# Six heads of batch 0 by the hardware queues, two by GpSimd's, and a re-ordered opening in a kernel of cross attention and a gated feed-forward layer

## The chip, the cores and the metric

The kernel runs on one core of one Trainium2 chip. The metric is device time in microseconds (us) for one execution. The core has five engines that run their own instruction streams side by side: TensorE (PE: matmuls and transposes), VectorE (DVE), ScalarE (ACT), GpSimd (POOL) and SyncE (SP, which here only issues transfers). Transfers (DMA) are issued by SP and ACT on the hardware queues (hardware_dynamic in the profile) and by POOL on the software queue (software_dynamic). In this kernel only POOL's transfers convert from float32 to bfloat16 on their way.

## What is computed

x is 8 batches x 8 heads x 512 rows x 64, state is 8 x 8 x 32 x 64. Two cross attentions share their scores, and what they give goes through a feed-forward layer with a rectified gate:

```python
scores = scale * np.matmul(x, state.transpose(0, 1, 3, 2))
a = softmax(scores)                       # over the 32 states
xread = np.matmul(a, state)
scores2 = scale * np.matmul(state, x.transpose(0, 1, 3, 2))
a2 = softmax(scores2)                     # over the 512 rows
sread = np.matmul(a2, x)
attn_out = np.concatenate([xread, sread], axis=2)
...
x = attn_out.transpose(0, 2, 1, 3).reshape(B * S, H * D)     # 4352 x 512
gate = np.maximum(x @ w_gate, 0.0)        # 512 x 1536
val = x @ w_val                           # 512 x 1536
return gate * val @ w_out                 # 1536 x 512
```

(softmax stands here for the reference's subtraction of the maximum, exponential and division.)

## The kernel before, in words

A batch's 512 rows lie as 128 partitions x 4 rows, for 8 heads of 64 columns. For each batch the kernel needs xT, the transpose of x in 16 blocks of 128 x 128 (two blocks for each head), and stT, the transposed states. Scores (att_sc, sc.b.jp) are matmuls of xT blocks with stT for four heads at a time, jp = 0 for heads 0 to 3 and jp = 1 for heads 4 to 7. ACT takes the exponential of each (att_exp, ex.b.jp, L206), DVE sums it and takes the reciprocal (att_sum, nr.b.jp, L212 and L214) and scales (att_scale, nx.b.jp, L218). The result is transposed again (aT, copied by ao) to be one operand of the feed-forward matmuls. The other operand is U, the product of state and weights (c_unit, c.b.lo.n for small pieces, copied to U by co at L320), so that gate and val come from one pair of matmuls over U (gv, L325), followed by ACT's rectifier (re, L354), DVE's product (mu, L358) and the output matmuls (o, L367).

The order of the first stretch is written out by hand. The text called program is a list of words, each of which emits the instructions of one step; for each engine they come in the order of the words that use it. A word such as xT.0.8.4@4 means step xT with arguments 0, 8, 4 (batch 0, blocks 8 to 11, that is heads 4 and 5) into PSUM bank 4. The steps that matter here:

- spin.1.n: one matmul of n columns (512 if not given) whose result nobody uses; spin32.2 is two of them in float32 at the very start.
- stc, stT, sto: states to bfloat16 (L118), transpose on PE (L123), copy out (L140).
- xc.0.j.eng: heads 2j and 2j+1 of batch 0 from the float32 tile xf to the bfloat16 tile xb, on engine eng (x_conv_pair, L144).
- xT.b.lo.n: n blocks of xb transposed on PE into PSUM (x_T, L162); xo.b.lo.n.eng: those blocks copied from PSUM to xT on engine eng (x_out, L165).
- sc, ex, nr, nx: as above. dx.b.part.parts: a part of batch b's x by POOL's queue (x_load, L441). dw: a piece of the gate or value weights by POOL's queue (w_dma, L109).

Ahead of the program stand the first transfers: on SP heads 0 and 1 in float32 and then a small one, touch, which reads 96 pieces of 32 bytes out of x into a tile that nothing reads; on ACT the states of the first batches and then heads 2 and 3 in float32; on POOL heads 4 to 7 with conversion, straight into xb. Then POOL makes the identity for the transposes and issues batch 1 in two halves, and after that weights, batch 2, the other states and the output weights. After the program a loop over groups of 128 feed-forward columns runs for the rest of the kernel, which the change leaves alone. The tile hs_sb (spare is its flat view) is first written long after the opening.

Of the kernel before, what the change touches and what calls it, by code (L numbers as in the profile page):

```python
# [8 lines left out]
FP32 = mybir.dt.float32  # L9
# [7 lines left out]
def kernel(  # L17
# [9 lines left out]
    nc = tc.nc  # L27

    B, H, S, D = x.shape
# [4 lines left out]
    NC = S // 128  # L34
# [3 lines left out]
    def pool(name, bufs, space=None):  # L38
        if space is None:
            return ctx.enter_context(tc.tile_pool(name=name, bufs=bufs))  # L40
        return ctx.enter_context(tc.tile_pool(name=name, bufs=bufs, space=space))

    const = pool("const", 1)
    upool = pool("upool", 3)
    xin = pool("xin", 1)
    att = pool("att", 2)
    small = pool("small", 4)
    anspool = pool("anspool", 3)
# [5 lines left out]

    NK = 2
    HK = H // NK


    wg_sb = const.tile([128, NJ, d_ff], BF16, name="wg_sb")
# [12 lines left out]
    spare = hs_sb.rearrange("p f n -> p (f n)")  # L72
# [5 lines left out]
    xf, xb, xT, eT, e_sn, a_sn, ANS, U, hsb = {}, {}, {}, {}, {}, {}, {}, {}, {}  # L78
# [18 lines left out]
    def state_dma(eng, lo, hi):  # L97
        src = state.rearrange("(g b) h (m i) d -> (b h m) g i d", b=2, i=4)
        eng.dma_start(out=st_f[:, lo // 2:hi // 2], in_=src[:, lo // 2:hi // 2])

    def place(h):

        return h // NJ, h % NJ ^ h // NJ

    def xb_alloc(b):
        xb[b] = att.tile([128, H, NC, D], BF16, name="xb", tag="xb", bufs=4)
# [75 lines left out]
    def sT_mm(b):  # L182

        held["sT", b] = [bank("sT_ps"), bank("sT_ps")]
        for kc in range(NK):
            for h in range(HK * kc, HK * kc + HK):
                j = place(h)[1]
# [62 lines left out]
    def x_pad(b):  # L250

        v = xa[:, b % NX].rearrange("p (c h) d -> p h c d", c=NC)[:, :, :, 0:D]
        for hs in (slice(0, HK), slice(HK, H)):
            nc.gpsimd.tensor_copy(out=v[:, hs], in_=xb[b][:, hs])  # L254
# [156 lines left out]

    ctx.enter_context(tc.manual_schedule())
    nc.vector.memset(stT, 0.0)
    xf[0] = xin.tile([128, HK, NC, D], FP32, name="xf", tag="xf")
    touch = const.tile([96, 1, 8], FP32, name="touch")

    def touch_dma(k, src, lo, n, step):
        v = src.rearrange("(a r) c -> a r c", r=step)[lo:lo + n, 0, 0:8]
        nc.sync.dma_start(out=touch[0:n, k], in_=v)

    for eng, j in ((nc.sync, 0), (nc.scalar, None), (nc.scalar, 1)):
        if j is None:
            state_dma(eng, 0, 2)
        else:
            src = x[0, 2 * j:2 * j + 2].rearrange("h (p c) d -> p h c d", c=NC)
            eng.dma_start(out=xf[0][:, 2 * j:2 * j + 2], in_=src)
    touch_dma(0, x.rearrange("b h s d -> (b h s) d"), 32, 96, 64)
    nc.scalar.activation(out=tiny, in_=nc.const_aps.tensor(0.0, (128, 1), FP32), func=AF.Exp)

    def w_load(w, lo, n):  # L430
        w_dma((moe_w_gate, moe_w_val)[w], (wg_sb, wv_sb)[w], lo, lo + n)

    xb_alloc(0)
    nc.gpsimd.dma_start(out=xb[0][:, HK:H], in_=x[0, HK:H].rearrange("h (p c) d -> p h c d", c=NC))
    make_identity(nc, id128)

    def x_load(b, part, parts):
# [13 lines left out]
    def x_load_behind(b, gb, gj):  # L451
# [11 lines left out]
    dx.1.0.2 dx.1.1.2 stc.0.1.dve stc.0.0.dve dw.0.0.128 dw.1.0.128 dw.0.128.128 dw.1.128.128 dw.0.256.256  # L463
    dw.1.256.256 dw.0.512.256 spin32.2 stT.0@0 dw.1.512.256 dw.0.768.256 dw.1.768.256 dw.0.1024.256 dw.1.1024.256
    dw.0.1280.256 dw.1.1280.256 dx.2.0.1 ds do.0.6 xc.0.0.act spin.1.256 xT.0.0.4@1 xc.0.1.dve sto.0.0.act
    spin.1.128 xT.0.4.4@2 xo.0.0.4.dve sto.0.1.dve xo.0.4.4.act spin.1 sc.0.0@3 ex.0.0 nr.0.0 spin.1.384
        xT.0.8.4@4 xT.0.12.4@5 xo.0.8.4.act xo.0.12.4.act spin.1 xT.1.0.8@6 sc.0.1@1 ex.0.1 xo.1.0.8.dve spin.1
    sc.1.0@0 xT.1.8.8@2 stc.1.1.pool stc.1.0.pool do.6.12 spin.1 c.0.0.128@34 nx.0.0 ex.1.0 nr.0.1 xo.1.8.8.act on
    stc.2.0.pool stc.3.1.pool co.0.0.128.0.act co.0.0.128.1.act spin.1 sc.1.1@5 nx.0.1 nr.1.0 aT.0.1@6 aT.0.0@1
    ex.1.1 c.1.128.128@02 ao.0.0.dve ao.0.1.act c.0.128.128@34 c.1.0.128@51 co.0.128.128.0.act gv.0.0@63  # L470
    co.1.128.128.1.act co.0.128.128.1.act re.0.0 co.1.128.128.0.act gv.0.1@72 nr.1.1 nx.1.0 co.1.0.128.1.act re.0.1
# [89 lines left out]
    for g in range(first, NF * (B + 1)):  # L561
        b, jf = divmod(g, NF)
# [47 lines left out]
```

## Time and profile before

| What | us |
|---|---|
| Three timed runs | 219.24, 220.28, 220.39 (median 220.28) |
| The profiled execution | 219.11 |
| its span, first to last instruction | 217.3 |
| PE busy | 209.4 |
| DVE busy | 134.8 |
| ACT busy | 117.8 |
| POOL busy | 42.5 |

The page of the profile gives busy times and shares of the span, the chain that ended last (followed back from the last instruction to what released it), the costliest groups of instructions, and for each transfer the time from its issue to its landing. In a timeline each line is: start, length, engine, line of the code, operation, out<-in, shapes, count; in brackets the engine's idle time before it and what ended it. An ended wait for several things is put down to the last of them. Lines such as L165 belong to a helper that several steps share. The granted clock of PE over the span was 0.998 of full speed.

### The profile page before, as it was taken

Reading aid. Unit: us, or ns where it says so; the run is one execution under the profiler, and the core shown is the slowest. Engines: PE = TensorE matmul, PEld = TensorE weight load, DVE = VectorE, ACT = ScalarE, POOL = GpSimd, SP = SyncE. Lnnn points to the kernel's source line nnn. Section 1 sums busy time; section 2 is a strip of 40 time slices with the busy share of each in tenths; the row PEclk is TensorE's granted clock in tenths of the full one; section 3 lists DMA queues with packets and bytes.
Section 4 is the critical chain, followed back from the end, with each engine's and each line's share of the span. In section 5 each row is a group of like instructions: output and inputs, shape, how many; then the busy total and the mean of one; then the engine's idle time right before and its main releaser. Section 6 shows DMA issues by size and latency. Waiting matters only on the chain.

```text
span 217.3 us, 4841 instructions
## 1 busy us (share of the span) xinstructions
PE 209.4 (96%) x1926; PEld 104.4 (48%) x1952; DVE 134.8 (62%) x233; ACT 117.8 (54%) x225; POOL 42.5 (20%) x63
## 2 busy tenths in 40 slices
PE   8799999999999999999999999999999999999994
PEld 4554454444444444444444444444544445666544
DVE  5799967956887778557966796388745444222100
ACT  4798887737546556455555656454646443333221
POOL 7964059005500431020107000000000000000000
PEclk9999999999999999999999999999999999999999
DMA  7999999488963996919391553131311122222132
GB/s 168 183 195 197 198 230 181 63 148 183 153 170 83 140 163 132 164 52 193 100 148 60 112 132 97 49 99 50 84 28 51 48 48 50 59 58 80 51 97 97
DMA packets 47511, 24.96 MB, mean 115 GB/s; under 512 B 27936, under 2 KB 43168, under 8 KB 47488
## 3 DMA queue, kind: packets, MB, share of 16 engines
q0 software_dynamic: 16896, 9.05, 30.8%
q1 hardware_dynamic: 29696, 14.85, 29.5%
q10 hardware_dynamic: 896, 0.75, 1.4%
q8 instruction: 15, 0.25, 0.5%
q14 instruction: 8, 0.07, 0.1%
HBM read 18.35 MB, written 8.91 MB: 125 GB/s over the span
## 4 chain that ended last, share of the span: by engine, by line
PE 93%; DMA 2%; issue 2%; ACT 1%; DVE 0%; POOL 0%; POOLq 0%
PE o_ps L367 39%; PE gv_ps L325 38%; PE gv_ps L347 5%; PE up L298 4%; DMA xb<-in_x_dram 2%; PE upc L298 2%; PE o_ps L396 1%; PE sr_ps L265 1%; PE sT_ps L189 1%; PE xT_ps L162 1%; PE sc_ps L179 1%; ACT xT L165 0%; PE aT_ps L234 0%; DVE xT L165 0%; ACT e_sn L206 0%
## 5 line engine op out<-in xcount | busy, mean ns | idle before, releaser
L367 PE MATMUL o_ps<-wo_sb,h_sb 128*128 128x512 bf16 x354 | 90.6, 379 | 2.4 <-issue 2.2
L325 PE MATMUL gv_ps<-ans,U 128*128 128x512 bf16 x377 | 92.5, 379 | 0.3
L358 DVE TENSOR_TENSOR h_sb<-gv_ps,g_sb 128x512 bf16<-128x512 f32 x96 | 65.0, 688 | 42.9 <-ACT g_sb L354 41.4
L354 ACT ACTIVATE g_sb<-gv_ps 128x512 bf16<-128x512 f32 (+1 forms) x108 | 61.8, 578 | 51.4 <-PE gv_ps L325 39.2
L325 PEld LDWEIGHTS <-U 128*128 128x128 bf16 x384 | 37.1, 98 | 44.6 <-issue 0.8
L367 PEld LDWEIGHTS <-h_sb 128*128 128x128 bf16 x372 | 35.2, 98 | 42.0 <-issue 4.0
L310 DVE CAST U<-up 128x512 bf16<-128x512 f32 x44 | 27.7, 683 | 5.7 <-PE up L298 5.7
L375 ACT COPY o_sb<-o_ps 128x512 f32<-128x512 f32 x31 | 18.4, 594 | 19.7 <-PE o_ps L367 16.7
L310 ACT CAST U<-up 128x512 bf16<-128x512 f32 x28 | 14.7, 596 | 8.8 <-PE up L298 8.8
L254 POOL COPY xa<-xb 128x1024 bf16<-128x1024 bf16 x16 | 16.0, 1044 | 10.4 <-PE sr_ps L265 5.9
L358 DVE TENSOR_TENSOR hs_sb<-gv_ps,g_sb 128x256 bf16<-128x256 f32 x12 | 5.1, 424 | 15.3 <-PE gv_ps L347 10.4
L212 DVE TENSOR_REDUCE cs<-e_sn 128x16 f32<-128x512 bf16 x16 | 10.8, 675 | 1.2 <-ACT e_sn L206 1.2
L218 DVE TENSOR_TENSOR a_sn<-e_sn,rc 128x512 bf16<-128x512 bf16 x16 | 10.9, 686 | 0.4
L298 PEld LDWEIGHTS <-stT 64*32 64x32 bf16 x560 | 6.8, 91 | 6.4 <-issue 5.3
L320 ACT CAST U<-upc 128x512 bf16<-128x512 f32 (+1 forms) x19 | 8.7, 523 | 1.7 <-PE upc L298 1.7
L453 POOL COPY mark<-g_sb 128x1 bf16<-128x1 bf16 x4 | 0.8, 190 | 41.4 <-ACT g_sb L354 41.4
L197 ACT ACTIVATE eT<-sT_ps 128x512 bf16<-128x512 f32 x10 | 5.4, 594 | 5.2 <-PE sT_ps L189 5.2
L441 POOL DMA_DIRECT2D xb<-in_x_dram x8 | 6.8, 850 | 2.9 <-issue 1.4
L347 PE MATMUL gv_ps<-br,wg_sb 128*128 128x256 bf16 x48 | 7.2, 273 | 0.1
L347 PE MATMUL gv_ps<-br,wv_sb 128*128 128x256 bf16 x48 | 7.2, 273 | 0.0
L399 DVE COPY o_sb<-o_ps 128x64 f32<-128x64 f32 x2 | 0.4, 224 | 10.6 <-PE o_ps L396 10.5
L298 PE MATMUL up<-wg_sb,stT 64*32 64x512 bf16 (+1 forms) x168 | 6.9, 348 | 0.0
(59 smaller groups left out, 122.7 us busy)
## 6 DMA issues: line engine op xcount, KB each, us to landing
out_dram<-o_sb SPq DMA_DIRECT2D x26, 256.0 KB, 2.4
xb<-in_x_dram POOLq DMA_DIRECT2D x6, 512.0 KB, 7.4
wo_sb<-in_moe_w_out_dram POOLq DMA_DIRECT2D x2, 768.0 KB, 10.7
out_dram<-o_sb SPq DMA_DIRECT2D x11, 128.0 KB, 2.3
wg_sb<-in_moe_w_gate_dram POOLq DMA_DIRECT2D x5, 256.0 KB, 9.1
wv_sb<-in_moe_w_val_dram POOLq DMA_DIRECT2D x5, 256.0 KB, 9.7
xb<-in_x_dram POOLq DMA_DIRECT2D x3, 256.0 KB, 5.1
st_f<-in_state_dram POOLq DMA_DIRECT2D x1, 384.0 KB, 11.5
```

Of the source, the lines that this page charges most:

```text
L212: nc.vector.reduce_sum(out=cs, in_=e_v, axis=AX.X)
L218: {"dve": nc.vector, "pool": nc.gpsimd}[eng].tensor_tensor(out=a_sn[b][:, jp].rearrange("p c (j n) -> p c j n", n=Ns), in0=e_v, in1=held[" ...
L254: nc.gpsimd.tensor_copy(out=v[:, hs], in_=xb[b][:, hs])
L298: nc.tensor.matmul(dst[kc][i0:i0 + 32], stT[r:r + 64, parity, b, h], wsb[r:r + 64, j, lo:lo + n], start=True, stop=True)
L310: copy[eng](out=U[b][:, w, kc, lo:lo + 512], in_=held["u", b, w, lo][kc])
L320: copy[eng](out=U[b][:, :, kc, lo:lo + n], in_=held["c", b, lo][kc])
L325: nc.tensor.matmul(ps[w], U[b][:, w, kc, f0:f0 + 128], ANS[b][:, kc].rearrange("p c t -> p (c t)"), start=(kc == 0), stop=(kc == NK - 1))
L347: nc.tensor.matmul(ps[w][:, 0:nt], wsb[:, j, f0:f0 + 128], br[:, j].rearrange("p b n -> p (b n)"), start=(j == 0), stop=(j == NJ - 1))
L354: nc.scalar.activation(out=g_sb[:, 0:n], in_=ps[0][:, 0:n], func=AF.Relu)
L358: nc.vector.tensor_tensor(out=dst, in0=ps[1][:, 0:n], in1=held["g", b, jf][:, 0:n], op=ALU.mult)
L367: nc.tensor.matmul(held["o", b, tsub], src[:, jf, tsub * 128:(tsub + 1) * 128], wo_sb[:, jf], start=(jf == 0), stop=(jf == NF - 1))
L375: copy[eng](out=o_sb, in_=held["o", b, tsub])
```

## The change

The float32 tile xf takes six heads instead of four (HX = HK + 2 = 6) and lies in the room of hs_sb instead of a pool of its own. SP issues head 0, head 1, and heads 4 and 5 as three transfers; touch is gone. ACT issues the states and heads 2 and 3, as before. POOL's first transfer has heads 6 and 7 only. In the program DVE gets one more conversion (xc.0.2, heads 4 and 5). The blocks of heads 4 and 5 and of heads 6 and 7 are transposed in two steps with a spin between, and the first are copied out by DVE instead of ACT. The transposes of the first half of batch 1 (xT.1.0.8) come behind the scores of heads 4 to 7 of batch 0 (sc.0.1) instead of ahead of them, and are copied out by ACT instead of DVE. DVE's scaling nx.0.0 stands earlier in the text, which leaves its place among DVE's instructions behind nr.0.0. One spin has 512 columns instead of 384.

```diff
-    xin = pool("xin", 1)
...
+    HX = HK + 2
...
-    xf[0] = xin.tile([128, HK, NC, D], FP32, name="xf", tag="xf")
-    touch = const.tile([96, 1, 8], FP32, name="touch")
+    xf[0] = spare.bitcast(FP32).rearrange("p (h c d) -> p h c d", h=HX, c=NC)
 
-    def touch_dma(k, src, lo, n, step):
-        v = src.rearrange("(a r) c -> a r c", r=step)[lo:lo + n, 0, 0:8]
-        nc.sync.dma_start(out=touch[0:n, k], in_=v)
-
-    for eng, j in ((nc.sync, 0), (nc.scalar, None), (nc.scalar, 1)):
-        if j is None:
-            state_dma(eng, 0, 2)
-        else:
-            src = x[0, 2 * j:2 * j + 2].rearrange("h (p c) d -> p h c d", c=NC)
-            eng.dma_start(out=xf[0][:, 2 * j:2 * j + 2], in_=src)
-    touch_dma(0, x.rearrange("b h s d -> (b h s) d"), 32, 96, 64)
+    def x32_load(eng, lo, hi):
+        eng.dma_start(out=xf[0][:, lo:hi], in_=x[0, lo:hi].rearrange("h (p c) d -> p h c d", c=NC))
+
+    x32_load(nc.sync, 0, 1)
+    state_dma(nc.scalar, 0, 2)
+    x32_load(nc.sync, 1, 2)
+    x32_load(nc.scalar, 2, 4)
+    x32_load(nc.sync, 4, HX)
...
-    nc.gpsimd.dma_start(out=xb[0][:, HK:H], in_=x[0, HK:H].rearrange("h (p c) d -> p h c d", c=NC))
+    nc.gpsimd.dma_start(out=xb[0][:, HX:H], in_=x[0, HX:H].rearrange("h (p c) d -> p h c d", c=NC))
...
-    spin.1.128 xT.0.4.4@2 xo.0.0.4.dve sto.0.1.dve xo.0.4.4.act spin.1 sc.0.0@3 ex.0.0 nr.0.0 spin.1.384
-        xT.0.8.4@4 xT.0.12.4@5 xo.0.8.4.act xo.0.12.4.act spin.1 xT.1.0.8@6 sc.0.1@1 ex.0.1 xo.1.0.8.dve spin.1
-    sc.1.0@0 xT.1.8.8@2 stc.1.1.pool stc.1.0.pool do.6.12 spin.1 c.0.0.128@34 nx.0.0 ex.1.0 nr.0.1 xo.1.8.8.act on
+    spin.1.128 xT.0.4.4@2 xo.0.0.4.dve sto.0.1.dve xo.0.4.4.act xc.0.2.dve spin.1 sc.0.0@3 ex.0.0 xT.0.8.4@4 xo.0.8.4.dve nr.0.0
+    spin.1 xT.0.12.4@5 xo.0.12.4.act spin.1 sc.0.1@1 xT.1.0.8@6 ex.0.1 nx.0.0 xo.1.0.8.act spin.1
+    sc.1.0@0 xT.1.8.8@2 stc.1.1.pool stc.1.0.pool do.6.12 spin.1 c.0.0.128@34 ex.1.0 nr.0.1 xo.1.8.8.act on
```

## The prediction

> **What bounds the kernel now.** I read first the shares of the engines and of the chain that ended last, then who makes TensorE (PE) wait after the opening, and then the opening itself.
>
> ```profile
> PE 209.4 (96%) x1926; PEld 104.4 (48%) x1952; DVE 134.8 (62%) x233; ACT 117.8 (54%) x225; POOL 42.5 (20%) x63
> PE 93%; DMA 2%; issue 2%; ACT 1%; DVE 0%; POOL 0%; POOLq 0%
> ```
>
> The second line is not a busy share: it is the chain followed back from the last instruction, and 93% of it is matmul. The view of PE's waits, asked for 11 us to the end, has one line:
>
> ```profile
> PE o_ps L367 <- issue: 2.2, 14, 0.2
> ```
>
> So from 11 us on PE waits for no other engine and no transfer. Whatever the opening gains or loses goes through to the end undiminished, and the opening is where all of the change lies. The chain of waits in order of time, 2.66 to 11.19 us, shows what sets the moment at which PE becomes dense (start, length, what):
>
> ```profile
> 2.66 5.08 DMA xb<-in_x_dram
> ...
> 7.79 0.64 PE xT_ps L162 x8
> ...
> 8.44 0.70 DVE xT L165
> ...
> 9.19 0.42 PE sc_ps L179 x8
> ...
> 9.64 0.60 ACT e_sn L206
> 10.23 0.91 ACT xT L165
> ...
> 11.19 0.41 PE sc_ps L179 x8
> ```
>
> The first half of batch 1 lands at 2.66 + 5.08 = 7.74. PE transposes it (xT.1.0.8), VectorE (DVE) copies it out, PE scores it (sc.1.0), ScalarE (ACT) takes the exponential and then the copy of the other half, and sc.1.1 starts at 11.19. The dense stretch begins there. The other end of the opening is batch 0, in the timeline of DVE, ACT and PE:
>
> ```profile
> 4.87 0.43 DVE L144 CAST xb<-xf 128x512 bf16<-128x512 f32 x1 [0.98 <-DMA xf<-in_x_dram]
> 5.32 0.42 DVE L165 COPY xT<-xT_ps 128x512 bf16<-128x512 bf16 x1
> 5.78 0.43 DVE L140 COPY stT<-stT_ps 64x512 bf16<-64x512 bf16 x1
> 6.26 0.45 PE L179 MATMUL sc_ps<-stT,xT 128*128 128x64 bf16 x8 [0.30 <-DVE stT L140]
> 7.24 1.07 ACT L165 COPY xT<-xT_ps 128x512 bf16<-128x512 bf16 x2
> 8.70 0.60 ACT L206 ACTIVATE e_sn<-sc_ps 128x512 bf16<-128x512 f32 x1 [0.38 <-PE sc_ps L179]
> ```
>
> sc.0.0 at 6.26 hangs on DVE's row of three, and this on the transposes of heads 0 and 1, which PE does at 4.90 behind its start-up matmuls. ex.0.1 at 8.70 comes so late only because sc.0.1 stands in PE's order behind xT.1.0.8, which waits until 7.74.
>
> **The order after the change, with unchanged arrivals.** Suppose heads 0 to 3 are there as now, so that sc.0.0 stays at 6.26 and ex.0.0 ends at 7.35. DVE: the added conversion xc.0.2 (0.43, the row of 4.87) 6.24 to 6.67, behind sto.0.1. PE: xT.0.8.4 from 6.70, done at 7.05. DVE: xo.0.8.4 (0.42) to 7.48, inside the 1.17 us that DVE idled before 7.38. PE: a start-up matmul (0.2), xT.0.12.4, done at 7.4. ACT: xo.0.12.4 (0.58) to 8.0. PE: last scores of sc.0.1 at 8.05, done 8.35. ACT: ex.0.1 at 8.39, 0.31 before the 8.70 of now. That is what the new order gains: batch 0 no longer queues behind batch 1. PE: xT.1.0.8 at 8.2, done by 8.8 (landed at 7.74, so no wait).
>
> Now the loss. The copy xo.1.0.8 goes from DVE (0.69 for 128x1024) to ACT, where the same shape shows 1.01, or 0.91 net of the overlap with the instruction before. On ACT it stands behind ex.0.1: 8.89 to 9.89. Then sc.1.0 at 9.94 (now 9.19), done 10.35; ex.1.0 at 10.39 (now 9.64); xo.1.8.8 10.88 to 11.89; sc.1.1 at 11.94 against 11.19, so **+0.75**. Before, DVE copied the first half of batch 1 while ACT did ex.0.1; after, ACT does ex, copy, ex, copy in one row with PE's scores between. DVE, relieved, has a_sn ready earlier than now (by about 10.8 against 11.34), but the transposes that want it (aT) stand behind sc.1.1 in PE's order, so this saves nothing. Behind sc.1.1 everything keeps its distances: co.0.0.128 follows xo.1.8.8 on ACT at once as now, and the gv matmuls follow 1.6 us after sc.1.1 as now (12.79).
>
> **The arrivals.** The page gives the time from issue to landing of the first transfers:
>
> ```profile
> xf<-in_x_dram SPq DMA_DIRECT2D x1, 256.0 KB, 3.2
> xf<-in_x_dram ACTq DMA_DIRECT2D x1, 256.0 KB, 3.6
> ...
> st_f<-in_state_dram ACTq DMA_DIRECT2D x1, 128.0 KB, 2.6
> ...
> touch<-in_x_dram SPq DMA_DIRECT2D x1, 3.0 KB, 3.4
> ```
>
> Heads 0 and 1 were SyncE's (SP's) first transfer, issued at 0.73 and landed at 3.9. They become its first and second, and ACT's conversion xc.0.0 needs both. An issue takes SP 0.46, so the second goes out at about 1.2. Bounds for its landing: 1.2 + 2.6 = 3.8, if it goes like the state's first 128 KB, and 1.2 + 3.6 = 4.8, if it goes like ACT's second. The nearest row is the transfer that now stands at its very place, second on SP, issued at 1.25: touch, 3.4 us although it is only 3 KB. I take 1.2 + 3.4, with some hundredths for the data: 4.65. Then xc.0.0 is 4.68 to 5.30 (0.62), the transposes of heads 0 and 1 run 5.36 to 5.75 instead of 4.90 to 5.29, and DVE's two copies end at 6.65 instead of 6.21: sc.0.0 at 6.70, **+0.45**, which passes through all steps above. At 3.8 it costs nothing, since PE is busy till 4.75 and the conversion would end before; at 4.8 it costs 0.6. It cannot gain: PE's 4.90 is set by the start-up matmuls.
>
> The Trainium skill has another price: "DMA: Bandwidth & Descriptors", section "Anatomy of one DMA — SWDGE (gpsimd) path", fits 2.0 us fixed plus bytes over 436 GB/s, given for GpSimd's path. By it, as an estimate, the second head would land at 3.5 and the sum would be +0.75, which is rival A's; the 3 KB that took 3.4 us do not agree with it here, so I stay with the row.
>
> Heads 2 and 3 (ACT's second, as now) landed at 4.8. They share now with more of SP's bytes: in the windows of 0.5 us the transfers move 305, 383 and 354 GB/s from 2.5 to 4.0, so there is little to spare. Nothing is lost up to 5.3 when heads 0 and 1 are late as taken; half a transfer's worth of sharing (0.3 us) stays below that. Heads 4 and 5 are SP's third, issued at about 1.7. Like touch they would land at 5.1; the successive landings on one queue are 0.7 (SP) and 1.5 us (ACT) apart, which puts them at 5.4 to 6.2; and POOL's transfer of heads 4 to 7 now lands at 1.24 + 5.1 = 6.3. DVE wants them at 6.7 by the sum. I take no wait; the bound above is +0.4 if they land at 7.1. Heads 6 and 7 by POOL, half of what it has now, come no later than 6.3 and are wanted at about 7.5. POOL's order is else unchanged; the identity follows its first transfer as now, at 2.7, wanted at 4.32. Batch 1 and the weights carry the same bytes in front of them; the removed touch, 3 KB, gives them under 0.1 us. The first wv_sb piece lands at 4.91 + 5.6 = 10.5 and is used at 10.55, so even an earlier front would stop there. Nothing queues behind SP's third issue: its next instruction is a transpose that waits for DVE long after. xf in the room of hs_sb, and 128 columns more of start-up matmul (under 0.1 us, in a stretch where PE waits), cost nothing.
>
> **The sum.** 0.75 + 0.45 = +1.2 us. The profiled execution took 219.11 us (span 217.3 and 1.8 around it): 220.3. The three runs shown have a median of 220.28, 1.2 above the profiled one, so the forecast for the median is 221.5. Their spread, 219.24 to 220.39, is 0.5%; about that much a measurement of this kernel can't tell from no change.
>
> **Rivals.** (A) The second head comes as soon as the first transfer did, or heads 0 and 1 are no later than 4.1: then only ACT's row counts, +0.75, 221.0. For it: the state's 2.6 us. Against: both second transfers took 3.4 and more. Chance 0.30.
>
> (B) Not slower. The timed runs are 1.2 us longer than the profiled one; if that is because the weights come later there, PE waits for them behind sc.1.1 whatever the opening does, and the delay disappears in that wait. The place is the second wv_sb piece (issued 6.37 + 5.6 = 12.0, used at 12.07); the point from which it decides is weights later by 1.2 us than profiled; then the time is 220.3, or 220.2 with touch's share gone. Against it: the profile shows not one such wait. Chance 0.10.
>
> (C) The heads on SP do not come sooner than by POOL, the third landing at 7.1: 0.4 more, +1.6, 221.9. Chance 0.13.
>
> (D) PE waits 0.9 us before sc.1.0 and 0.7 before sc.1.1 instead of 0.53 and 0.07, and the granted clock falls. It stayed at full with PE busy 2.51 of 3.40 us (7.4 to 10.8), which speaks against it. If some 3.4 us of dense work (the length of that window) then ran at the pace of the state's transposes at 4.32 (311 ns each, against 219 for the same shape later), that would cost 3.4 x (1 - 219/311) = 1.0 more: 222.5. Chance 0.05. The Trainium skill, "TensorE: Matmul & The Clock Gate", Part 1, sets the fall at an idle window of about 3.4 us, which no gap here comes near.
>
> **Numbers.** Forecast 0.42, A 0.30, B 0.10, C 0.13, D 0.05. Range 219.9 to 222.8: it holds the forecast, A and C with the spread of runs (0.5 us either way), most of B and D, and leaves the tails out. Slower by over 0.5% (above 221.4): half of the forecast and somewhat over, a quarter of A, nearly all of C and D, 0.52. Faster by over 0.5% has no mechanism here but noise and a front I misread: 0.08. Within: 0.40.
>
> **What would show it.** Right: ACT's xT copy of 128x1024 twice, with sc.1.0 and sc.1.1 waiting for ACT xT; sc.1.1 near 12.4; xc.0.0 starting at 4.6 or later; no new PE wait after it. Wrong: sc.1.1 at or before 11.2, PE waiting for wv_sb behind it, xc.0.0 at 3.97, or a PE wait for DVE's third conversion.

## The result, and the profile after

| What | us |
|---|---|
| Timed, before: median of 10 runs (219.24 to 220.54) | 220.21 |
| Timed, after: median of 10 runs (220.72 to 223.10) | 221.26 |
| Ratio after to before, 95% interval | 1.0061 [1.0035, 1.0088] |
| Profiled execution after (span) | 220.74 (219.0) |
| Profiled execution before (span) | 219.11 (217.3) |

The change makes the kernel slower by 0.6%, 1.3 us by the ratio and 1.05 us by the medians. The two profiled executions lie 1.63 us apart. Both are early ones: the one of before lies 1.1 us under the median of its runs (the eighth run below asks why), and the one of after, 220.74, is the second lowest of its ten.

The shares of the engines and of the chain that ended last, after:

```profile
PE 210.1 (96%) x1926; PEld 104.7 (48%) x1952; DVE 135.6 (62%) x234; ACT 118.4 (54%) x225; POOL 42.6 (19%) x63
PE 92%; DMA 2%; ACT 2%; issue 2%; SPq 0%; DVE 0%
```

PE still fills the chain; ACT has come up from 1% to 2%. What makes PE wait from 10 us to the end, after (engine and line, for whom: us in total, times, longest):

```profile
PE o_ps L367 <- issue: 2.2, 14, 0.2
PE sc_ps L179 <- ACT xT L165: 1.5, 2, 1.1
```

The second line is new: sc.1.0 and sc.1.1 wait for ACT's copies of batch 1. After them PE waits for no other engine and no transfer, as before. The first gv matmul starts at 14.45 instead of 12.79, and from it to the end of the span it is 204.5 us in both. The whole difference is made in the opening. Its chain, after (start, length, what):

```profile
1.65 5.24 DMA hs_sb<-in_x_dram
...
6.92 0.50 DVE xb L144
...
7.46 0.40 PE xT_ps L162 x4
...
8.34 0.59 ACT xT L165
...
9.30 0.60 ACT e_sn L206
9.90 0.91 ACT xT L165
...
10.86 0.42 PE sc_ps L179 x8
...
11.30 0.60 ACT e_sn L206
11.90 0.91 ACT xT L165
...
12.86 0.41 PE sc_ps L179 x8
```

Two things stand in it that were not in the chain of before. It begins with heads 4 and 5 of batch 0 (SP's third transfer, landed at 1.65 + 5.24 = 6.89) instead of batch 1's first half; and from ex.0.1 at 9.30 it runs ex, copy, ex, copy on ACT, 3.56 us to sc.1.1, where before it took 2.49 (8.70 to 11.19). The times to landing of the float32 heads, after:

```profile
hs_sb<-in_x_dram SPq DMA_DIRECT2D x2, 128.0 KB, 2.7
hs_sb<-in_x_dram ACTq DMA_DIRECT2D x1, 256.0 KB, 3.5
hs_sb<-in_x_dram SPq DMA_DIRECT2D x1, 256.0 KB, 5.2
```

Heads 0 and 1 took 2.7 us each, though the second is SP's second transfer; the third, of twice the size, took 5.2. ACT's timeline confirms that heads 0 and 1 came in time: xc.0.0 starts as before, at 3.97.

```profile
3.97 0.62 ACT L144 CAST xb<-hs_sb 128x512 bf16<-128x512 f32 x1 [0.80 <-DMA hs_sb<-in_x_dram]
```

PE's timeline, after, shows how much of the opening's delay is a wait for heads 4 and 5:

```profile
4.96 0.63 PE L162 MATMUL xT_ps<-id,xb 128*128 128x128 bf16 x4
...
6.57 0.53 PE L179 MATMUL sc_ps<-stT,xT 128*128 128x64 bf16 x8
7.46 0.40 PE L162 MATMUL xT_ps<-id,xb 128*128 128x128 bf16 x4 [0.37 <-DVE xb L144]
```

In the profile of before the same four transposes of the first line were:

```profile
4.90 0.39 PE L162 MATMUL xT_ps<-id,xb 128*128 128x128 bf16 x4
```

They are those of heads 0 and 1. They take 311 ns each in this execution and took 219 ns in that of before, although the views of both give the granted clock there as 1.00. So sc.0.0 starts at 6.57 instead of 6.26, and PE is busy until 7.10. The start of xT.0.8.4 at 7.46 is set by heads 4 and 5, as the chain says, but only the last 0.37 us are a wait of PE: had these heads come in time, it would have started near 7.10 in this execution. The kernel before has such late starts too in other executions (sc.0.0 at 6.57 in run 3, which lacks only touch, and 6.50 in run 8). There sc.1.1 waits for batch 1 or the weights, which come later, and the slow start does not show in the time.

### The profile page after: what moved, and what is told of

It is laid out like the page before. It is cut to its first block, busy times and chain, and to the rows that moved or that the text cites. A ratio compares the mean times of both kernels' runs of the same rounds, so it can differ in the third digit from the quotient of the medians.

```text
span 219.0 us, 4846 instructions
## 1 busy us (share of the span) xinstructions
PE 210.1 (96%) x1926; PEld 104.7 (48%) x1952; DVE 135.6 (62%) x234; ACT 118.4 (54%) x225; POOL 42.6 (19%) x63
## 4 chain that ended last, share of the span: by engine, by line
PE 92%; DMA 2%; ACT 2%; issue 2%; SPq 0%; DVE 0%
PE o_ps L367 39%; PE gv_ps L325 38%; PE gv_ps L347 5%; PE up L298 4%; DMA hs_sb<-in_x_dram 2%; PE upc L298 2%; PE o_ps L396 1%; PE sr_ps L265 1%; ACT xT L165 1%; PE sc_ps L179 1%; PE sT_ps L189 1%; PE xT_ps L162 1%; ACT e_sn L206 1%; PE aT_ps L234 0%; SPq L417 0%
```

## The experiments

Each kernel was timed beside the kernel before on the same chip; ratios are to before. In each profile I read the landing of the heads, the starts of ex.0.1 (ACT) and sc.1.1 (PE), and the first gv matmul. One sum holds in all of them: the first gv matmul starts 1.59 to 1.60 us after sc.1.1, and 204.4 to 204.6 us later the span ends. So the time of an execution is the start of sc.1.1 plus 207.8 to 208.0 us in all fourteen profiles.

### 1. The order alone: after's order of steps, before's transfers

```diff
 (before.py, with the program of after)
-    ... xo.0.4.4.act xc.0.2.dve spin.1 sc.0.0@3 ...
+    ... xo.0.4.4.act spin.1 sc.0.0@3 ...
```

> The new order of steps with the transfers of before (heads 4 to 7 by GpSimd's queue, touch kept, no third conversion). Theory 'both': the changed kernel's +1.6 us in the profile is part late heads 4 and 5 (landed at 6.89 on SP's queue), part the copy of batch 1's first half in ScalarE's row. Then here heads 4 to 7 land near 6.35, PE does not wait for them, ex.0.1 starts near 8.4, sc.1.1 near 11.9 (11.19 before, 12.86 changed), time +0.75 us over before. Rival 'transfers only': the order itself is harmless, sc.1.1 at 11.2 or earlier, time within 0.2 us of before. Rival 'order only': sc.1.1 near 12.9 as in the changed kernel, +1.6.

Measured: 1.0021 [1.0006, 1.0036], +0.5 us. Heads 4 to 7 landed at 7.05, ex.0.1 8.94, sc.1.1 12.50: 3.56 from one to the other, the length of the changed kernel's row. The order costs time by itself, less than the whole. The chain to ex.0.1 does not lead back to heads 4 to 7 in this run. It leads through PE's start-up matmuls and the transposes of heads 0 and 1 (314 ns each) to sc.0.0, which ends at 7.10, and xT.0.8.4 starts at once. The heads are not cleared by that: they landed 0.05 before, so that PE's slow start and the late heads meet here, and either alone would have given this ex.0.1. That heads 4 to 7 landed at 7.05 and not near 6.35, with the transfers of before, was the first sign that GpSimd's stream differs from one execution to the next.

### 2. The transfers alone: after's transfers, before's order

```diff
 (after.py, with the program of before)
-    ... xo.0.4.4.act spin.1 sc.0.0@3 ex.0.0 nr.0.0 spin.1.384
+    ... xo.0.4.4.act xc.0.2.dve spin.1 sc.0.0@3 ex.0.0 nr.0.0 spin.1.384
```

> The new transfers (and the third conversion on VectorE, which they need) with the order of steps of before. Theory 'both': heads 4 and 5 land near 6.9 again, xc.0.2 ends near 7.4, the scores sc.0.1 come near 9.0 and sc.1.1 near 11.9: +0.7 us over before. Rival 'order only': sc.1.1 at 11.2 to 11.4, no change in time. Rival 'transfers only': sc.1.1 near 12.9, +1.6.

Measured: 1.0010 [0.9988, 1.0032], not told from no change. Heads 4 and 5 landed at 6.92, as late as in the changed kernel, but batch 1's first half landed at 8.78, and sc.1.1 came at 12.24, 3.45 us after that. The chain before sc.1.1 in this run:

```profile
4.85 6.73 DMA wv_sb<-in_moe_w_val_dram
...
11.62 0.25 PE upc L298 x8
11.87 0.32 PE warm_ps L443
...
12.23 0.41 PE sc_ps L179 x8
```

It does not lead back to heads 4 and 5 at all, but to the first value weights, which stand in PE's order ahead of sc.1.1. In the old order the late heads lie beside the wait for batch 1. So neither part alone costs what both cost: +0.5 and +0.2, together +1.3. Whether both cost more than the sum of the two, the intervals do not tell.

### 3. Before without touch

```diff
-    touch_dma(0, x.rearrange("b h s d -> (b h s) d"), 32, 96, 64)
```

> Before without its small transfer touch and nothing else. In the changed kernel all later transfers landed 0.6 to 0.7 us later than before (batch 1's first half 8.35 against 7.74, the second wv_sb piece 12.62 against 12.03), though they have the same bytes in front of them. Theory 'touch': reading 96 small pieces of x early makes the later reads of the same region start faster; without it batch 1 lands at 8.2 to 8.4 here too, xT.1.0.8 waits for it, sc.1.1 near 11.7, +0.5 us. Rival 'sharing': touch is only 3 KB in the way; batch 1 lands at 7.7 or a little earlier, time within 0.2 us of before.

Measured: 0.9995 [0.9981, 1.0010]. Batch 1 landed at 8.50 and sc.1.1 came at 11.96, as theory 'touch' said of the profile, and yet the time was that of before, as 'sharing' said. Both hold together only if before too usually runs with batch 1 at about 8.5, which the eighth run asks.

### 4. After with touch put back

```diff
     x32_load(nc.sync, 4, HX)
+    touch_dma(nc.scalar, 0, x.rearrange("b h s d -> (b h s) d"), 32, 96, 64)
```

> The changed kernel with touch put back, as ScalarE's third transfer. Theory 'touch': heads 4 and 5 land near 6.2 or earlier instead of 6.89 and batch 1's first half near 7.8 instead of 8.35; sc.1.1 near 12.0 to 12.2 instead of 12.86, time 0.7 us under the changed kernel, that is +0.4 to +0.8 over before. Rival 'sharing': heads 4 and 5 land at 6.9 or later, time as the changed kernel's, +1.0 to +1.6 over before.

Measured: 1.0058 [1.0036, 1.0081], as the changed kernel. Heads 4 and 5 landed at 6.84, batch 1's first half at 8.65, sc.1.1 at 12.82. Theory 'touch' falls by these landings (6.84 where it had 6.2, 8.65 where it had 7.8); the time by itself would not decide, since the median lies 0.8 over before and the ratio gives 1.3. Two things more stand in this trace. The chain leads back not to heads 4 and 5 but to heads 2 and 3, which landed at 5.62. And touch, third on ACT's queue, took 5.3 us to land, where as SP's second it had taken 3.4: 3 KB as a third transfer came as late as 256 KB, so the size is not what makes it late here.

### 5. After with the copy of batch 1's first half on VectorE again

```diff
-    ... ex.0.1 nx.0.0 xo.1.0.8.act spin.1
+    ... ex.0.1 xo.1.0.8.dve nx.0.0 spin.1
```

> The changed kernel with one copy moved back: xo.1.0.8 on VectorE, ahead of nx.0.0, instead of on ScalarE. Theory 'ScalarE's row': from ex.0.1 to sc.1.1 the changed kernel takes 3.56 us, the kernel before (and before without touch) 2.5; with the copy on VectorE sc.1.0 starts as soon as xT.1.0.8 is copied, near 10.5 instead of 10.86, sc.1.1 near 12.45 instead of 12.86; the aT transposes then wait a little for VectorE's nx.0.1 (near 12.8), so the gv matmuls start near 14.2 instead of 14.45 and the time falls by 0.2 to 0.4 us against the changed kernel. Rival 'late heads only': the copy's engine does not matter because PE's order behind the late heads 4 and 5 sets everything: sc.1.1 within 0.1 of 12.86, no change.

Measured: 1.0060 [1.0031, 1.0089], no gain in time that these five runs can show. In this profile heads 4 and 5 landed at 7.56, so the absolute times are not comparable, but the row is. Its chain:

```profile
9.96 0.46 PE xT_ps L162 x8
...
10.44 0.70 DVE xT L165
...
11.64 0.60 ACT e_sn L206
12.23 0.91 ACT xT L165
...
13.19 0.41 PE sc_ps L179 x8
```

The copy takes 0.70 on DVE and starts as soon as PE's transposes end at 10.42; on ACT it took 0.91 and waited for ex.0.1. From ex.0.1 (10.00) to sc.1.1 it is 3.20 us, against 3.56 with ACT's copy (the changed kernel and runs 1, 4 and 6) and 2.49 to 2.52 in the old order (before, and runs 2, 3 and 8). So 0.36 of the row's 1.05 us is the copy's engine, and 0.69 is PE's order: xT.1.0.8 and its copy now begin only behind sc.0.1, where before they were done beside it. In the profile of this run PE waits 1.14 us for heads 4 and 5 ahead of xT.0.8.4.

### 6. After with heads 0 and 1 in one transfer

```diff
-    x32_load(nc.sync, 0, 1)
+    x32_load(nc.sync, 0, 2)
...
-    x32_load(nc.sync, 1, 2)
```

> The changed kernel with heads 0 and 1 in one transfer on SP, so that heads 4 and 5 are SP's second transfer (issued near 1.2) instead of its third (1.65). Theory 'late start': SP's third transfer moves its first packets only near 4.0, when GpSimd's stream starts and shares the engines, and so lands at 6.9; as second it starts near 3.4 and lands near 5.2. Then heads 6 and 7 (near 7) come last, ex.0.1 starts near 8.5 instead of 9.30, sc.1.1 near 12.1, time 0.7 us under the changed kernel. Rival 'sharing': any third stream next to GpSimd's is slow; heads 4 and 5 land at 6.5 or later, time as the changed kernel's.

Measured: 1.0046 [1.0029, 1.0063], four runs. The times to landing in this run:

```profile
hs_sb<-in_x_dram SPq DMA_DIRECT2D x2, 256.0 KB, 3.8
hs_sb<-in_x_dram ACTq DMA_DIRECT2D x1, 256.0 KB, 4.1
```

As SP's second transfer heads 4 and 5 landed at 5.53, 1.4 us sooner than as its third: the landing is what theory 'late start' said, though its reason, the start of GpSimd's stream, is not shown by it. But heads 2 and 3 came at 5.31 instead of 4.70, their conversion held up DVE's whole row, xc.0.2 ran at 6.69, and ex.0.1 came at 9.26. The wait moved from one pair of heads to the other and nothing was gained on the path (sc.1.1 12.81). That it is this run's change that made heads 2 and 3 late is not shown: with heads 0 to 5 issued as in the changed kernel they landed at 5.50 in run 2 and 5.62 in run 4.

### 7. Both of these undone

The edits of runs 5 and 6 in one kernel.

> Both edits of the two runs above in one: heads 0 and 1 in one transfer, xo.1.0.8 on VectorE. If the two causes are separate and complete, heads 4 and 5 land near 5.2, sc.1.0 comes near 9.8, sc.1.1 near 11.8, gv near 13.4, and the time is that of before within 0.2 us or slightly under it. If something else in the change costs time, it stays 0.5 us or more over before.

Measured: 1.0026 [1.0013, 1.0038], +0.6 us. Heads 4 and 5 landed at 5.78, heads 2 and 3 at 5.60 (4.84 to 4.88 in the two profiles of before), ex.0.1 9.25, sc.1.1 12.44, 3.20 later. Run 6 has the same transfers and the copy on ACT, and ex.0.1 at the same moment (9.26): sc.1.1 came 0.37 later there, and its median is 220.80 against 220.42 here. That is the copy's engine alone, in the trace and in the time. About half of the loss is gone; what stays is PE's order and the pair of heads that comes late.

### 8. Before, profiled again

> The kernel before, profiled a second time. In the profile shown first, batch 1's first half landed at 7.74 and sc.1.1 started at 11.19, with 219.11 us, lower than nearly all timed runs. Where heads 4 to 7 are unchanged on GpSimd's queue (order alone, before without touch) batch 1 landed at 8.4 to 8.5. If the first profile was an early one, this one shows batch 1 at 8.3 to 8.5, sc.1.1 near 11.9 and about 219.9 us; if not, 7.7, 11.2 and 219.1 again.

The chain of this execution:

```profile
2.67 6.29 DMA xb<-in_x_dram
...
9.01 0.64 PE xT_ps L162 x8
...
10.42 0.42 PE sc_ps L179 x8
...
12.41 0.41 PE sc_ps L179 x8
```

The same transfer took 6.29 us instead of 5.08; sc.1.1 comes 3.45 us after its landing in both. This execution took 220.32 us, 1.2 more than the first profile and 1.2 is also what sc.1.1 is later by (12.41 against 11.19). The first profile was an early one; timed medians of before in these comparisons lie at 219.74 to 220.21. Against a landing of about 8.5 (run 3), before starts sc.1.1 near 11.95, and the changed kernel's 12.86 is 0.9 later.

### 9. Heads 4 and 5 on ACT's queue, behind heads 2 and 3

```diff
-    x32_load(nc.sync, 4, HX)
+    x32_load(nc.scalar, 4, HX)
```

on top of run 7.

> The run with both undone (heads 0 and 1 in one transfer, xo.1.0.8 on VectorE), and heads 4 and 5 moved to ScalarE's queue behind heads 2 and 3. In the run with both undone heads 4 and 5 came early (5.8) but heads 2 and 3 late (5.60 against 4.84 to 4.88 before), so ex.0.1 stayed at 9.25. Theory 'queue mates': two heads that share the engines with another queue's heads come late, behind them on one queue they do not hurt them; heads 2 and 3 land near 4.9, 4 and 5 near 5.7, ex.0.1 near 8.8, sc.1.1 (3.2 us later) near 12.0, time within 0.2 us of before. Rival: the hardware queues together cannot bring six heads sooner; heads 2 and 3 still land at 5.3 or later and the time stays 0.4 to 0.6 over before.

Measured: 1.0010 [0.9989, 1.0032]. Heads 2 and 3 landed at 4.79, as expected, but heads 4 and 5 at 6.53, and ex.0.1 came at 9.26, not 8.8. The first half of the theory fits (heads 2 and 3 at 4.79, 4.83 and 4.72 here and in runs 10 and 12), though they also came at 4.66 to 4.74 with the changed kernel's transfers (after, runs 5 and 11). The second half falls: a third transfer is late on ACT's queue too (6.53 here, 7.55 and 7.40 in runs 10 and 12). In this run DVE's conversion of heads 4 and 5 also took 0.80 us, where the prediction had 0.43; why was not tested.

### 10. One start-up matmul less

```diff
-    spin.1 xT.0.12.4@5 xo.0.12.4.act spin.1 sc.0.1@1
+    xT.0.12.4@5 xo.0.12.4.act spin.1 sc.0.1@1
```

on top of run 9.

> The same without the start-up matmul between xT.0.8.4 and xT.0.12.4, which stands 0.22 us in PE's way there. If PE's row from the last of heads 4 to 7 to ex.0.1 is the path, ex.0.1 and sc.1.1 come 0.2 us sooner than in the run beside it, and the time is 0.2 us lower, at or just under before. If heads 6 and 7 (landing near 7 by GpSimd's queue) set it, nothing changes.

Measured: 1.0026 [1.0001, 1.0052]; the interval overlaps that of run 9, and no gain in time is seen. In the trace the row from xT.0.8.4 to ex.0.1 takes 1.65 us instead of 1.84 in run 9, so the start-up matmul did stand in the way, by about the 0.2 expected. The profiled execution (222.01 us) does not show what became of it: heads 4 and 5 landed at 7.55 instead of 6.53, and PE's granted clock fell (0.992 over the span), as in the next run.

### 11. After, profiled again

> The changed kernel, profiled a second time. If the reading holds, heads 4 and 5 land at 6.8 to 7.6, ex.0.1 comes 2.4 us after that, and sc.1.1 another 3.56 later, whatever GpSimd's stream does in this execution; the gv matmuls start 1.6 after sc.1.1.

This execution took 222.60 us. Heads 4 and 5 landed at 7.67. The waits and lengths then were not 2.4 and 3.56 but 3.09 and 3.92, and the reason is PE's clock. PE's timeline, and the view by windows of 3.41 us (span, PE, PEld, DVE, ACT and POOL busy, PE's granted clock, DMA share, GB/s):

```profile
8.18 0.61 PE L162 MATMUL xT_ps<-id,xb 128*128 128x128 bf16 x4 [1.49 <-DVE xb L144]
```

```profile
4.73:8.14 3.41, 1.48 (x23) 1.10 (x21) 1.68 (x4) 1.76 (x3) 3.41 (x6) 1.00 1.24 189
8.14:11.55 3.41, 3.33 (x26) 2.48 (x27) 2.12 (x5) 1.18 (x2) 2.49 (x4) 0.50 1.72 180
```

PE waited 1.49 us for the converted heads 4 and 5, was busy for 1.48 of 3.41 us, and for the next 3.41 us was granted half its clock, just while it worked through the opening's scores. Against the 2.41 and 3.56 of the first profile that cost 0.68 us up to ex.0.1 and 0.36 from there to sc.1.1.

### 12. Before's order with the best of the transfers

```diff
 (run 2, with)
-    x32_load(nc.sync, 0, 1)
+    x32_load(nc.sync, 0, 2)
...
-    x32_load(nc.sync, 1, 2)
...
-    x32_load(nc.sync, 4, HX)
+    x32_load(nc.scalar, 4, HX)
```

> The order of steps of before (with the third conversion), and six heads by the hardware queues in the arrangement that did best: heads 0 and 1 in one transfer on SP, heads 4 and 5 on ScalarE's queue behind heads 2 and 3. In this order sc.1.1 came 3.45 us after batch 1's first half landed in four profiles. Batch 1 has the same bytes in front of it, so it lands at 7.8 to 8.7 as in the others, sc.1.1 at 11.3 to 12.2 and the time is that of before within 0.2 us. Rival: with six heads off GpSimd's queue batch 1 itself comes sooner, below 7.7 every time, and the time falls 0.4 us or more under before. It would be slower only if heads 4 and 5 landed past 7.0.

Measured: 1.0002 [0.9993, 1.0012]. Batch 1's first half landed at 8.61, sc.1.1 came at 12.21, 3.60 us after that and not 3.45. The chain of this run leads back not to batch 1 but to heads 4 and 5, ACT's third transfer: they landed at 7.40, PE waited 1.38 us for their conversion, and xT.1.0.8 started at 8.81 behind their transposes, without a wait of its own. This execution (220.20 us) is among the slowest of the twelve. Six heads on the hardware queues gain nothing in the old order either: batch 1 comes no sooner, and heads 4 and 5 come about as late as it can bear. No version tried beats the kernel before.

## Why the prediction was right, and where it was not

The forecast, slower with 221.5 us, met 221.26. Of its two terms one was right on the path and stands in the traces; the other did not happen, and delays that the prediction put at nothing stood in its place.

**ACT's row, +0.75: the path was right, its length rightly summed, its cause right in part.** The prediction had 3.55 us from ex.0.1 to sc.1.1 (8.39 to 11.94); the trace has 3.56. The prediction put the cost on the copy's move to ACT; runs 5 to 7 show that this is 0.36 of it and that the larger 0.69 is PE's order. The gain set against it, ex.0.1 0.31 us before 8.70, did not come: ex.0.1 came at 9.30.

**Heads 0 and 1 late, +0.45: wrong.** The step that failed is the choice of touch, second on SP, as the row for the second head. The head landed at 3.89, 2.69 us after its issue and near the state's 2.6, the lower bound. The estimate from the Trainium skill ("DMA: Bandwidth & Descriptors", "Anatomy of one DMA — SWDGE (gpsimd) path"), 2.3 us after the issue, was closer to it than touch's 3.4. For the 256 KB of the third transfer the same fit gives 2.6 as an estimate, half of the 5.2 measured.

**sc.0.0 as early as before but for that, and heads 4 and 5 with no wait: both wrong.** In the changed kernel's first profile xT.0.8.4 starts at 7.46 instead of the 6.70 of the working, 0.76 late, and sc.1.1 at 12.86 instead of 11.94, 0.92 late; the other 0.16 lie in the steps between xT.0.8.4 and ex.0.1 (1.84 against 1.69) and in rounding. The 0.76 is set by heads 4 and 5, which landed at 6.89. About 0.4 of it would have come without them, since PE's slow start kept it busy with sc.0.0 until 7.10; the 0.37 beyond that is theirs alone. The prediction took PE's pace from one profile, in which it was fast early, and so put its share at nothing.

The prediction let heads 4 and 5 land at 5.4 to 6.2, wanted at 6.7, with +0.4 as the bound; in the five profiles with this arrangement they landed at 6.84 to 7.67. Heads 6 and 7, which were to come no later than 6.3, came at 7.06, without a wait. The late heads are rival C's mechanism, with 0.13 of the chance. Its price of 0.4 was counted on top of the 0.45 for heads 0 and 1. PE's wait for them was 0.37 us in the first profile, 1.14 in run 5 and 1.49 in the second profile of the changed kernel.

**Luck.** That the total came out near the median is in part chance: 0.92 of other delays stood where the forecast had 0.45, and the difference between profiles and medians, 1.10 before and 0.52 after, took about as much off again.

**The base.** The working stood on a profile with sc.1.1 at 11.19. Runs 3 and 8 have 11.96 and 12.41. Between the two first profiles the change costs 1.63 us, between the medians 1.05. Adding the sum to the median of the runs was right in form, but run 8 shows what the 1.2 us between the median and the profile are in one execution: GpSimd's stream comes later, and with it batch 1, for which the old order waits and the new one does not.

**The rivals.** A (only ACT's row, 221.0) had heads 0 and 1 right and missed the slow start and heads 4 and 5. B (the weights hide it) falls, since behind sc.1.1 PE waits for no weights after the change; but its guess at the base was near, for in runs 2, 3 and 8 the weights do come later, together with batch 1, and in runs 2 and 3 the chain to sc.1.1 leads back to them. D, the clock, given 0.05 and 1.0 us, happened in the second profile, where it cost 1.04 us. Of the ten timed runs one, the 223.10, has a mean granted clock of 0.992, the other nine 0.998 or more. In all, 7 of the 49 timed runs of after and runs 4, 5, 9 and 10 have a mean clock of 0.992 or less, against one of the 85 runs of before that were timed beside the experiments. These five versions join the new order with a third transfer of 256 KB.

**Costed at nothing, rightly:** touch (run 3: 0.9995 [0.9981, 1.0010]). The room of hs_sb and POOL's order were not tried by themselves; run 2 has both and gives 1.0010 [0.9988, 1.0032].

## What to carry to other kernels

Before taking a wait off a chain, ask what the next steps did beside it: here batch 1's transposes and their copy ran in the shadow of batch 0's scores, and putting batch 0 first laid them end to end, 1.05 us longer from ex.0.1 to sc.1.1. A queue's third transfer is not its second plus an issue time; take its price from a third one, and if there is none keep the bound in the forecast. And profile the kernel before twice when the change is about 0.5%: one execution's opening was 1.2 us away from the next. A delay that one order hides can be on the path of another: in the old order of runs 3 and 8 PE's slow start is not on the path to sc.1.1.

## What the runs showed of the hardware that I had not expected

- Third transfers of 256 KB at the start landed 4.9 to 6.0 us after their issue (SP: 5.2, 5.3, 5.2, 5.9, 6.0; ACT: 4.9, 5.9, 5.7), second ones of the same size 3.4 to 4.5. A third one of 3 KB took 5.3 us (run 4). GpSimd's stream was starting at that time; that the sharing with it is the cause was not shown by itself.
- The moment from which PE's 128x128 transposes take 219 ns instead of 311 to 314 differs between executions. In runs 4, 7 and 9 those at 4.3 us already took 219 to 230 ns; in the first profile of after and in runs 1, 3 and 10 those at 5.8 us still took 311 to 314. The view by windows gives the granted clock as 1.00 in all of this stretch, so it does not tell the two paces apart. What sets the moment was not tested.
- GpSimd's transfer of batch 1's first half took 5.08 and 6.29 us in two executions of the same kernel.
- PE's granted clock fell to half for 3.41 us after a window of 3.41 us in which PE had been busy for 1.48 us (run 11) and, in run 10, 2.02. In run 5 a window with 1.96 us and in the first profile of after one with 1.89 were followed by no fall, so PE's busy time, as the profile counts it, does not decide it alone. The Trainium skill ("TensorE: Matmul & The Clock Gate", Part 1) puts the fall after an idle window of about 3.4 us; the length of the window agrees, but here it was far from idle. Where the border lies these runs do not settle.
